# Retention and two feed-forward layers on one core: rooms for raw weight tiles, sums by DMA, scaling order

## The chip, the cores and the metric

The kernel runs on one core of one Trainium2 chip. The metric is the device time of one execution in microseconds. The core has a matrix engine (TensorE, PE in the rows, with its weight loads as PEld), a vector engine (VectorE, DVE), an activation engine (ScalarE, ACT), GpSimd (POOL), which here only issues DMAs, and SyncE (SP), which issues nearly all DMAs. Each engine works through its own queue in order and waits on semaphores.

## The reference

Everything is fp32. A retention (linear attention with a decaying state) over 4 batches, 8 heads, 768 positions and 64 features gives 3072 tokens of 512 features. They pass through two feed-forward layers of width 2048:

```python
state = gamma * state + k[t] (outer) v[t];  y[t] = scale * q[t] @ state
h = x @ w_in;  P = a0 + a1*h + a2*h**2 + a3*h**3
Q = 1 + |b0|*|h| + |b1|*h**2;  x = (P / (Q + 1e-6)) @ w_out        # layer 1
h = x @ w_in2;  out = (h * clip(h + 3, 0, 6) / 6) @ w_out2         # layer 2
```

## The kernel before

**Blocks and steps.** The 3072 tokens are cut into 6 blocks of 512 and the width 2048 into 16 units of 128. A step is one unit of one block in one layer: 96 steps per layer, 192 in all, written out one after the other (L653). Step n computes `h` of its unit with 12 matmuls (`emit_h`, L319), then the activation of the step before (`s1_h`, L393; `s1_pq`, L405; `s1_r`, L414; layer 2: `s2_h`, `s2_g`), the end of the activation of two steps before (`s1_g`, `s_hi`, `s_lo`), and last adds the result of two steps before into the accumulators of its block (`emit_o`, L331, 12 matmuls). fp32 accuracy comes from splitting every operand in two parts of the matrix engine's reduced fp32 type: xh and xl, gh and gl, and for weights the two halves of one `both` tile, hi and lo. The order of steps in layer 1 is block 0 units 0 to 7 (steps 0 to 7), block 1 units 0 to 15 (8 to 23), block 0 units 8 to 15 (24 to 31), then blocks 2 to 5; layer 2 has the same order.

**Attention.** Each block has four chunks of 128 tokens (`att_load` to `att_evac`). Block 0's run ahead of step 0. Block 1's are spread over steps 0 to 7, those of block 2 (VIA) over steps 8 to 22, one every four steps; their loads are issued at steps 7, 11, 15 and 19 into the tiles T, tq and kv, each once chunk c-1 has been read, and their result goes through DRAM (`x_via`). Blocks 0 and 1 (EARLY) have tiles a, b and r per chunk, 24 tiles in all, in the places that weights take later (`early_pair`).

**Weight tiles.** The weights of each layer are 32 tiles of 512 KB (wi and wo of 16 units), numbered by need: 0 = wi0, 1 = wi1, 2 = wo0, 3 = wi2, 4 = wo1 and so on; 16 and 17 are wi8 and wi9, 18 = wo8, 19 = wi10, 20 = wo9, 21 = wi11, up to 31; layer 2 has 32 to 63. A tile passes through these stages:

- `w_load` (L94): SP loads the raw tile into a room (L98 or L103; raw tiles are called rwi and rwo).
- `w_scale` (L109): ScalarE scales the upper half words in place (L111).
- `w_bits` (L115): VectorE puts the number together in three instructions (L119, L120, L123). L120 and L123 need the scaling; the trio is called the shift in this text.
- `w_hi` (L128): ScalarE writes hi (L131).
- lo = number minus hi, either by VectorE (L143), or for the tiles that `by_dma` names: ScalarE writes -hi into lo (`w_minus`, L135), and GpSimd issues a DMA that adds the number to it in place (L141). After it the room is free.

`w_first` does the shift and hi of a tile and calls the scaling of a later tile between them; `w_second` makes lo. Two tiles per step are made in steps 0 to 8 (0 to 2 ahead of them), one per step in steps 9 to 19 (tiles 21 to 31); `w_until` sets this. In the last 16 steps of layer 1 (80 to 95) the first tiles of layer 2 are made, one every second step. In a step VectorE's order is: lo of the last tile, the first shift, the activation of the step before, attention, the second shift; the lo of a tile stands at the beginning of the step after.

**Rooms.** Raw tiles lie in rooms: two `raw` tiles, and kv and T until step 5, when these go to block 2's attention (L694); at step 80 they come back. `w_ahead` (L507) issues loads at the end of each step while a room is free in the list; a load on SP's queue waits there until the lo of the tile that was in its room is done. The functions hold the limits: `w_scale_next(i + 2)` lets the scaling run one tile ahead of the shift, as far as the tile's load has been issued.

Of the kernel before, what the change touches and what calls it, by code (L numbers as in the profile page):

```python
# [7 lines left out]
F32 = mybir.dt.float32  # L8
F32R = mybir.dt.float32r
# [9 lines left out]
VIA = 2  # L19
CUT1, CUT2 = 8, 8  # L20
LAG = 2
SUMS = (3, 20)
WARM = 3
Q_CONST = 1.0 + 1e-6
LN_SCALE = 2.0**16
# [4 lines left out]
def tile_retention_moe_moe2(  # L30
# [19 lines left out]
    FT = DFF // 128  # L50
# [3 lines left out]

    ctx.enter_context(tc.manual_schedule())
    const = ctx.enter_context(tc.tile_pool(name="const", bufs=1))
    wts = ctx.enter_context(tc.tile_pool(name="wts", bufs=FT))
    raw_p = ctx.enter_context(tc.tile_pool(name="raw", bufs=2))
    x_p = ctx.enter_context(tc.tile_pool(name="xin", bufs=1))
    g_p = ctx.enter_context(tc.tile_pool(name="g", bufs=2))  # L60
# [24 lines left out]

    def pair_tile(tag, name):

        if tag == "raw":
            return raw_p.tile([128, 1024], F32, tag="raw", name=name)
        if tag == "T":  # L90
            return att.tile([128, 1536], F32, tag=tag, name=name)[:, 0:1024]
        return att.tile([128, 1024], F32, tag=tag, name=name)

    def w_load(tag, kind, layer, f):  # L94
        src = ((w_in1, w_in2) if kind == "wi" else (w_out1, w_out2))[layer].bitcast(I32)
        raw = pair_tile(tag, f"r{kind}{layer}_{f}").bitcast(I32)
        if kind == "wi":
            nc.sync.dma_start(  # L98
                out=raw.rearrange("p (c f) -> p c f", c=KD),
                in_=src[:, f * 256 : (f + 1) * 256].rearrange("(c p) f -> p c f", p=128),  # L100
            )
        else:
            nc.sync.dma_start(out=raw, in_=src[f * 128 : (f + 1) * 128, :])  # L103
        raws[kind, layer, f] = raw.rearrange("p (n t) -> p n t", t=2)
# [4 lines left out]
    def w_scale(kind, layer, f):  # L109
        hw = raws[kind, layer, f][:, :, 1].bitcast(F32)  # L110
        nc.scalar.activation(hw, hw, AF.Copy, scale=2.0**-112)  # L111
# [3 lines left out]
    def w_bits(kind, layer, f):  # L115
        raw = raws[kind, layer, f]
        lw, hw = raw[:, :, 0], raw[:, :, 1]
        z = raw.rearrange("p n t -> p (n t)")[:, 0:512]
        nc.vector.tensor_scalar(out=lw, in0=lw, scalar1=29, scalar2=None, op0=ALU.logical_shift_right)  # L119
        nc.vector.scalar_tensor_tensor(  # L120
            out=lw, in0=hw, scalar=-(2**31), in1=lw, op0=ALU.bitwise_and, op1=ALU.bitwise_or
        )
        nc.vector.scalar_tensor_tensor(  # L123
            out=z, in0=hw, scalar=3, in1=lw, op0=ALU.logical_shift_left, op1=ALU.bitwise_or
        )
        raws[kind, layer, f] = z.bitcast(F32)

    def w_hi(kind, layer, f):  # L128
        both = wts.tile([128, 1024], F32R, tag=kind, name=f"{kind}{layer}_{f}")
        weights[kind, layer, f] = (both[:, 0:512], both[:, 512:1024])  # L130
        nc.scalar.activation(weights[kind, layer, f][0], raws[kind, layer, f], AF.Copy)  # L131

    def w_minus(kind, layer, f):
        hi, lo = weights[kind, layer, f]
        nc.scalar.activation(lo, hi.bitcast(F32), AF.Copy, scale=-1.0)  # L135

    def w_lo(kind, layer, f, by_dma):
        hi, lo = weights[kind, layer, f]
        z = raws.pop((kind, layer, f))
        if by_dma:  # L140
            nc.gpsimd.dma_start(out=lo.bitcast(F32), in_=z, accum_op=ALU.add)  # L141
        else:
            nc.vector.tensor_tensor(out=lo, in0=z, in1=hi.bitcast(F32), op=ALU.subtract)  # L143
# [3 lines left out]
    loaded = {}  # L147
    attn = {}
    score = {}
    early = {"n": 0}  # L150

    def early_pair(name):

        early["n"] += 1
        tag = ("wi", "wo")[early["n"] % 2]
        return wts.tile([128, 1024], F32R, tag=tag, name=name).bitcast(F32)

    def heads(t):
        return t.rearrange("p (h d) -> p h d", h=H)
# [13 lines left out]
    def att_load(blk, c, parts=(0, 4, 1, 3, 2)):  # L173
        nm = f"{blk}_{c}"
        g = blk * CPB + c
        if (blk, c) not in loaded:
            if blk in EARLY:
                a, b, r = (early_pair(f"T{i}_{nm}") for i in "abr")
                q, tq, ka = a[:, 0:512], a[:, 512:1024], b
            else:  # L180
                t = att.tile([128, 1536], F32, tag="T", name=f"T{nm}")
                q, ka = t[:, 0:512], t[:, 512:1536]
                r = pair_tile("kv", f"kv{nm}")
                tq = att.tile([128, 512], F32, tag="tq", name=f"tq{nm}")
            loaded[blk, c] = [q, ka[:, 0:512], r[:, 0:512], r[:, 512:1024], tq, ka]
        for i in parts:
            if i == 4:
                src = tables[:, g % CPS * DM : (g % CPS + 1) * DM]
            else:
                src = (qk_t, kv)[i // 2][g, :, i % 2 * 512 : (i % 2 + 1) * 512]  # L190
            nc.sync.dma_start(out=loaded[blk, c][i], in_=src)
# [286 lines left out]
    def at_step(n):  # L478
        return steps[n] if 0 <= n < len(steps) else None
# [3 lines left out]
    for layer in range(2):  # L483
        need = []
        for f in range(FT):
            n = min(at_of[layer, b, f] for b in range(NBLK))
            need += [(n, "wi", layer, f), (n + LAG, "wo", layer, f)]
        jobs += [j[1:] for j in sorted(need, key=lambda j: j[0])]
    NW = 2 * FT
    made = {"load": 0, "scale": 0, "bits": 0, "lo": 0}  # L490
    free = ["raw", "raw", "kv", "T"]
    lent = {"kv": True, "T": True}
    held = {}

    def by_dma(i):
        return SUMS[0] <= i < SUMS[1]

    def w_until(n):

# [5 lines left out]
        return min(2 * NW, NW + 7 + (135 * (m + 1) + 99) // 100 if m < CUT2 else NW + 11 + m)  # L505

    def w_ahead(lim):  # L507
        while free and made["load"] < lim:
            i = made["load"]
            held[i] = free.pop(0)  # L510
            w_load(held[i], *jobs[i])
            made["load"] += 1

    def w_scale_next(lim):
        if made["scale"] < min(made["load"], lim):
            w_scale(*jobs[made["scale"]])
            made["scale"] += 1
# [3 lines left out]
    def w_first():  # L521
        i = made["bits"]
        if made["scale"] == i:
            w_ahead(i + 1)
            w_scale_next(i + 1)
        w_bits(*jobs[i])
        w_scale_next(i + 2)
        w_hi(*jobs[i])
        if by_dma(i):
            w_minus(*jobs[i])  # L530
        made["bits"] += 1

    def w_second():
        if made["lo"] < made["bits"]:
            i = made["lo"]
            w_lo(*jobs[i], by_dma(i))
            tag = held.pop(i)
            if lent.get(tag, True):
                free.append(tag)
            made["lo"] += 1  # L540


# [22 lines left out]
    for key in (VIA, *range(NBLK, 2 * NBLK)):  # L565
        n = at_of[0, key, 0] if key < NBLK else at_of[1, key - NBLK, 0]
# [58 lines left out]
    w_bits(*jobs[0])  # L625
    made["bits"] = 1
    w_hi(*jobs[0])
    att_q(0, 3)
    att_scores(0, 3)
# [23 lines left out]
    for n in range(len(steps) + LAG):  # L653
        cur, k1, k2 = (at_step(n - i) for i in range(3))
        todo = w_until(n) - made["bits"]
        if cur:
            emit_h(cur)
        for fn, *args in begun:
            fn(*args)
        begun.clear()  # L660
        if k1:
            (s1_h, s2_h)[k1[0]](k1)
        for key in late:
            if key[:2] not in partial and key[0] == 0:
                emit_evac(*key)
        for fn, *args in begin.get(n, ()):
            fn(*args)
        if k2 and k2[0] == 0:
            s1_g(k2)
            s_hi(k2)  # L670
        elif k2:
            s_lo(k2)
        for key in late:
            if key[:2] in acc:
                emit_evac(*key)
        late.clear()
        while made["lo"] < made["bits"]:
            w_second()
        rest = (lambda: s_lo(k2)) if k2 and k2[0] == 0 else None
        if k1 and k1[0] == 1:  # L680
            if rest:
                rest()
            s2_g(k1)
            s_hi(k1)
        if todo > 0:
            w_first()
        if k1 and k1[0] == 0:
            s1_pq(k1, rest)
            s1_r(k1)
        if todo > 1:  # L690
            w_second()
        for fn, *args in before.get(n, ()):
            fn(*args)
        if n == CUT1 - 3:  # L694
            lent.update(kv=False, T=False)
            free[:] = [t for t in free if t == "raw"]
        if n == N1 - FT:
            lent.clear()
            free += ["kv", "T"]
        if todo > 1:  # L700
            w_first()
        w_ahead(NW if n < N1 - FT else 2 * NW)
        o = at_step(n - LAG)
        if o:
            emit_o(o)
            if o[2] == ends[o][1]:
                late.append(o)
        for fn, *args in after.get(n, ()):
            fn(*args)
        if cur and cur[1:] == (0, FT - 1):  # L710
            sum_load(*cur[:2])
# [71 lines left out]
```

## Time and profile before

| | us |
|---|---|
| median of 3 runs | 1224.5 (1223.58 to 1227.64) |
| profiled execution, its own time | 1225.62 |
| its span, first to last instruction | 1223.6 |
| TensorE busy | 1158.8 (95%) |
| VectorE busy | 813.4 (66%) |
| ScalarE busy | 617.3 (50%) |
| GpSimd busy | 15.4 (1%), 23 instructions |

The shares are means over stretches that have different limits, so the rows below go by stretches. A row of an order of time gives start, duration, engine, line, operation, the tile written and the tiles read; the bracket at its end is the idle time of the engine before it and what ended that.

### The profile page before, as it was taken

The page shows a single profiled execution, that of the slowest core. Times are in us where ns is not written, and L with a number is a line of the kernel's source. Part 1 is how long each engine was busy: PE and PEld are TensorE (multiplying, and loading weights), DVE is VectorE, ACT ScalarE, POOL GpSimd, SP SyncE. Part 2 cuts the span into 40 slices and gives each one's busy share as a digit, 9 for nine tenths or more (in the row PEclk, how much of TensorE's full clock was granted, in tenths as well). Part 3 has the DMA queues.
Part 4 walks back from the last instruction along what each step waited for, and adds up shares of the span by engine and source line. Part 5 has one row for each costly group of instructions (what it writes and reads, how often), then busy time and mean ns, then how long its engine had stood idle before and what let it go on. Part 6 is the DMA issues. An engine that isn't in the chain of part 4 may idle for free.

```text
span 1223.6 us, 15677 instructions
## 1 busy us (share of the span) xinstructions
PE 1158.8 (95%) x6022; PEld 936.2 (77%) x6022; DVE 813.4 (66%) x1264; ACT 617.3 (50%) x1003; POOL 15.4 (1%) x23
## 2 busy tenths in 40 slices
PE   6776888999999999999999899999999999999998
PEld 5554666788888888888776688888888888888886
DVE  6897889999888888887899997643323232332222
ACT  2576656686666666655777665433222222222222
POOL 0111000000000000000000000000000000000000
PEclk8898899999999999999999999999999999999999
DMA  9776433231211221212121264302100100100000
GB/s 333 221 180 155 136 97 104 76 132 52 70 44 44 78 87 44 78 44 81 67 78 43 69 207 138 103 1 86 61 9 1 61 9 1 61 9 1 35 1 35
DMA packets 57099, 95.74 MB, mean 78 GB/s; under 512 B 5057, under 2 KB 23617, under 8 KB 57025
## 3 DMA queue, kind: packets, MB, share of 16 engines
q1 hardware_dynamic: 54576, 90.29, 22.5%
q0 software_dynamic: 2448, 4.46, 2.2%
q8 instruction: 47, 0.77, 0.3%
q14 instruction: 28, 0.22, 0.1%
HBM read 74.54 MB, written 15.73 MB: 74 GB/s over the span
## 4 chain that ended last, share of the span: by engine, by line
PE 74%; DVE 14%; ACT 4%; DMA 4%; issue 3%; SPq 0%; DVEq 0%; ACTq 0%; POOLq 0%
PE h L328 35%; PE accA L352 18%; PE accB L352 18%; DMA rwo<-in_moe_w_out_dram 2%; PE sc L216 1%; DVE p L408 1%; DVE u L423 1%; PE py L247 1%; DVE p L424 1%; DVE u L409 1%; DVE rwo L120 1%; DVE p L412 1%; DVE rwi L120 1%; DVE p L425 1%; DMA wi<-rwi 1%
## 5 line engine op out<-in xcount | busy, mean ns | idle before, releaser
L328 PE MATMUL h<-xh,wi 128*128 128x512 f32 x1536 | 418.7, 395 | 0.7 <-ACT xh L303 0.7
L328 PEld LDWEIGHTS h<-xh,wi 128*128 128x128 f32 x1536 | 287.2, 189 | 65.0 <-issue 3.2
L328 PE MATMUL h<-xl,wi 128*128 128x512 f32 x768 | 206.1, 390 | 0.0
L448 DVE SCALAR_TENSOR_TENSOR g<-r,h 128x512 f32<-128x512 f32 x96 | 66.0, 688 | 164.6 <-ACT r L442 164.1
L328 PEld LDWEIGHTS h<-xl,wi 128*128 128x128 f32 x768 | 144.7, 188 | 31.0
L442 ACT ACTIVATE r<-h,cst 128x512 f32<-128x512 f32 x96 | 65.9, 686 | 178.1 <-PE h L328 177.5
L352 PE MATMUL accA<-gh,wo 128*128 128x512 f32 x384 | 122.5, 401 | 20.7 <-ACT gh L430 20.7
L436 DVE TENSOR_TENSOR gl<-g,gh 128x512 fp32r<-128x512 f32 x96 | 66.4, 692 | 112.3 <-ACT gh L430 112.3
L430 ACT ACTIVATE gh<-g 128x512 fp32r<-128x512 f32 x96 | 60.8, 633 | 150.5 <-PE accB L352 116.6
L352 PE MATMUL accB<-gh,wo 128*128 128x512 f32 x384 | 120.8, 396 | 0.0
L352 PE MATMUL accA<-wo,gh 128*128 128x512 f32 x384 | 118.3, 389 | 0.0
L352 PE MATMUL accB<-wo,gh 128*128 128x512 f32 x384 | 118.2, 389 | 0.0
L352 PEld LDWEIGHTS accA<-gh,wo 128*128 128x128 f32 x384 | 71.5, 191 | 41.4 <-ACT gh L430 26.6
L417 ACT ACTIVATE r<-u,cst 128x512 f32<-128x512 f32 x96 | 69.3, 722 | 54.6 <-DVE u L409 54.6
L400 ACT ACTIVATE p<-h,ab 128x512 f32<-128x512 f32 x96 | 74.3, 774 | 38.9 <-PE h L328 36.7
L436 DVE TENSOR_TENSOR gl<-p,gh 128x512 fp32r<-128x512 f32 x96 | 65.7, 685 | 32.3 <-ACT gh L430 32.1
L352 PEld LDWEIGHTS accB<-gh,wo 128*128 128x128 f32 x384 | 73.6, 192 | 15.8
L352 PEld LDWEIGHTS accA<-wo,gh 128*128 128x128 f32 x384 | 72.1, 188 | 15.0
L352 PEld LDWEIGHTS accB<-wo,gh 128*128 128x128 f32 x384 | 72.1, 188 | 14.9
L352 PE MATMUL accA<-gl,wo 128*128 128x512 f32 x192 | 64.2, 410 | 19.0 <-DVE gl L436 18.6
L430 ACT ACTIVATE gh<-p 128x512 fp32r<-128x512 f32 x96 | 60.7, 632 | 34.7 <-DVE p L425 34.6
L352 PE MATMUL accB<-wo,gl 128*128 128x512 f32 x192 | 74.8, 389 | 0.0
(77 smaller groups left out, 1468.3 us busy)
## 6 DMA issues: line engine op xcount, KB each, us to landing
rwi<-in_moe_w_in_dram SPq DMA_DIRECT2D x32, 512.0 KB, 3.8
rwo<-in_moe_w_out_dram SPq DMA_DIRECT2D x32, 512.0 KB, 3.5
T<-in_qk_t_dram SPq DMA_DIRECT2D x32, 256.0 KB, 3.9
kv<-in_kv_dram SPq DMA_DIRECT2D x32, 256.0 KB, 4.5
x<-o SPq DMA_DIRECT2D x24, 256.0 KB, 2.3
xr<-x SPq DMA_DIRECT2D x24, 256.0 KB, 3.7
out_dram<-o SPq DMA_DIRECT2D x20, 256.0 KB, 2.1
Tr<-in_kv_dram SPq DMA_DIRECT2D x16, 256.0 KB, 6.2
```

The costliest lines, as they stand in the source:

```text
L120: nc.vector.scalar_tensor_tensor(out=lw, in0=hw, scalar=-(2**31), in1=lw, op0=ALU.bitwise_and, op1=ALU.bitwise_or)
L216: nc.tensor.matmul(banks[e][:, p * CH : (p + 1) * CH], lhsT=kT[rows, p, :], rhs=qT[rows, p, :], start=True, stop=True)
L247: nc.tensor.matmul(to(e, j, i), lhsT=vr[:, 2 * p + e, :], rhs=am[:, e * NP + p, :], start=j == 0, stop=first and j == 1, skip_group_check= ...
L328: nc.tensor.matmul(ps, lhsT=w[:, cs], rhs=x[:, c, :], start=n == 0, stop=n == 3 * KD - 1)
L352: nc.tensor.matmul(acc[layer, blk][j], lhsT=l, rhs=r, start=f == f0 and i == 0, stop=f == f1 and i == 2)
L400: nc.scalar.activation(p, h, AF.Identity, scale=ab[:, 3:4], bias=ab[:, 2:3])
L408: nc.vector.tensor_tensor(out=p, in0=p, in1=h, op=ALU.mult)
L417: nc.scalar.activation(r, u, AF.Ln, scale=1.0 / LN_SCALE, bias=ln_bias)
L430: nc.scalar.activation(gh, tm[key], AF.Copy)
L436: nc.vector.tensor_tensor(out=gl, in0=tm.pop(key), in1=gh.bitcast(F32), op=ALU.subtract)
L442: nc.scalar.activation(r, hps[key], AF.Relu, bias=three)
L448: nc.vector.scalar_tensor_tensor(out=g, in0=r, scalar=6.0, in1=h, op0=ALU.min, op1=ALU.mult)
```

## The change

All weights have a place of their own: the pool had 16 buffers for wi and 16 for wo, used in turn, and has one each for 32 tags (wi0 to wo15). The early attention tiles lie in fixed places, from unit 8 on, and block 1's chunk c takes those of block 0's chunk c. The places of the last two units (wi14, wo14, wi15, wo15) hold raw tiles for loads 0 to 23, beside the two `raw` tiles: six rooms; kv and T are rooms only from step 80 on. Lo by DMA is used for tiles 3 to 25 and 32 to 39 (31 tiles) in place of 3 to 19 (17). `w_first` lets the scaling run up to i + 3, and after step 1 one more scaling is called, which puts it two tiles ahead of the shift.

```diff
-SUMS = (3, 20)
+SUMS = ((3, 26), (32, 40))
+EARLY_AT = 8
+SPARE, SPARE_TO = ("wi14", "wo14", "wi15", "wo15"), 24
-    wts = ctx.enter_context(tc.tile_pool(name="wts", bufs=FT))
+    wts = ctx.enter_context(tc.tile_pool(name="wts", bufs=1))
     def pair_tile(tag, name):
+        if tag in SPARE:
+            return wts.tile([128, 1024], F32R, tag=tag, name=name).bitcast(F32)
     def w_hi(kind, layer, f):
-        both = wts.tile([128, 1024], F32R, tag=kind, name=f"{kind}{layer}_{f}")
+        both = wts.tile([128, 1024], F32R, tag=f"{kind}{f}", name=f"{kind}{layer}_{f}")
-    def early_pair(name):
-        early["n"] += 1
-        tag = ("wi", "wo")[early["n"] % 2]
-        return wts.tile([128, 1024], F32R, tag=tag, name=name).bitcast(F32)
+    def early_pair(c, i, name):
+        n = 2 * EARLY_AT + 3 * c + i
+        return wts.tile([128, 1024], F32R, tag=f"{('wi', 'wo')[n % 2]}{n // 2}", name=name).bitcast(F32)
-    free = ["raw", "raw", "kv", "T"]
-    lent = {"kv": True, "T": True}
+    free = [*SPARE, "raw", "raw"]
     def by_dma(i):
-        return SUMS[0] <= i < SUMS[1]
+        return any(lo <= i < hi for lo, hi in SUMS)
     def w_ahead(lim):
-        while free and made["load"] < lim:
+        while made["load"] < lim:
             i = made["load"]
-            held[i] = free.pop(0)
+            rooms = [t for t in free if i < SPARE_TO or t not in SPARE]
+            if not rooms:
+                return
+            held[i] = rooms[0]
+            free.remove(rooms[0])
     def w_first():
...
-        w_scale_next(i + 2)
+        w_scale_next(i + 3)
     def w_second():
...
-            tag = held.pop(i)
-            if lent.get(tag, True):
-                free.append(tag)
+            free.append(held.pop(i))
...
-        if n == CUT1 - 3:
-            lent.update(kv=False, T=False)
-            free[:] = [t for t in free if t == "raw"]
         if n == N1 - FT:
-            lent.clear()
             free += ["kv", "T"]
         if todo > 1:
             w_first()
         w_ahead(NW if n < N1 - FT else 2 * NW)
+        if n == 1:
+            w_scale_next(NW)
```

## Rows read from the trace of the kernel before

**Rows 1.** Stretches: us, length, busy time and instructions per engine, clock, DMA.
```profile
29.58:107.30 77.72, 59.71 (x393) 45.15 (x393) 71.65 (x115) 54.71 (x94) 13.35 (x15) 0.91 0.75 197
107.30:160.00 52.70, 36.44 (x181) 27.04 (x179) 39.79 (x66) 29.95 (x50) 1.76 (x2) 0.84 0.49 145
160.00:240.00 80.00, 72.34 (x424) 55.50 (x425) 73.59 (x117) 50.10 (x83) 0.00 (x0) 0.96 0.26 80
240.00:600.00 360.00, 360.00 (x2111) 293.72 (x2110) 310.42 (x477) 235.28 (x381) 0.00 (x0) 1.00 0.21 69
600.00:700.00 100.00, 91.22 (x385) 70.15 (x384) 93.15 (x148) 71.30 (x119) 0.00 (x0) 1.00 0.20 64
```

**Rows 2.** Chain of waits, 95 to 160 us: start, us, what.
```profile
101.92 6.56 DMA wi<-rwi
108.53 3.58 DMA rwo<-in_moe_w_out_dram
...
134.75 2.56 PE accB L352 x6
...
150.47 5.53 DMA rwo<-in_moe_w_out_dram
```

**Rows 3.** VectorE in order of time, 104 to 160 us.
```profile
112.21 0.43 DVE L119 TENSOR_SCALAR rwo<-rwo 128x512 int32<-128x512 int32 x1 [4.50 <-DMA rwo<-in_moe_w_out_dram]
...
116.23 0.59 DVE L119 TENSOR_SCALAR rwi<-rwi 128x512 int32<-128x512 int32 x1
118.54 0.69 DVE L120 SCALAR_TENSOR_TENSOR rwi<-rwi 128x512 int32<-128x512 int32 x1 [1.72 <-ACT rwi L111]
...
127.46 0.68 DVE L143 TENSOR_TENSOR wo<-rwo,wo 128x512 fp32r<-128x512 f32 x1
128.63 0.44 DVE L119 TENSOR_SCALAR rwi<-rwi 128x512 int32<-128x512 int32 x1 [0.49 <-DMA rwi<-in_moe_w_in_dram]
...
139.53 0.69 DVE L120 SCALAR_TENSOR_TENSOR rwo<-rwo 128x512 int32<-128x512 int32 x1 [3.04 <-ACT rwo L111]
...
146.51 0.68 DVE L143 TENSOR_TENSOR wo<-rwo,wo 128x512 fp32r<-128x512 f32 x1
...
148.59 0.69 DVE L120 SCALAR_TENSOR_TENSOR rwi<-rwi 128x512 int32<-128x512 int32 x1 [1.06 <-ACT rwi L111]
...
156.03 0.43 DVE L119 TENSOR_SCALAR rwo<-rwo 128x512 int32<-128x512 int32 x1 [0.57 <-DMA rwo<-in_moe_w_out_dram]
```

**Rows 4.** GpSimd in order of time, the accumulating DMA of tile 12.
```profile
83.17 0.90 POOL L141 DMA_DIRECT2D wo<-rwo  x1 [5.82 <-ACT wo L135]
```

**Rows 5.** DMA issues: tile, queue, count, KB each, median us to landing.
```profile
wo<-rwo POOLq DMA_DIRECT2D x8, 256.0 KB, 4.4
```

**Rows 6.** Chain of waits, 0 to 300 us: one subtraction.
```profile
220.72 0.60 DVE wo L143
```

**Rows 7.** Line 135: count, ns min/median/max, first and last start.
```profile
L135 ACT ACTIVATE wi<-wi x9: 630/632/636, 37.5 to 120.7; 128x512 fp32r<-128x512 f32 x9
```

**Rows 8.** All engines in order of time, 606 to 622 us: ScalarE's logarithm.
```profile
618.95 0.72 ACT L417 ACTIVATE r<-u,cst 128x512 f32<-128x512 f32 x1 [0.69 <-DVE u L409]
```

**Rows 9.** TensorE in order of time, 128 to 152 us.
```profile
132.67 0.79 PE L352 MATMUL accA<-gl,wo 128*128 128x512 f32 x1 [2.87 <-DVE gl L436]
...
144.66 1.09 PE L247 MATMUL py<-T,kv 128*64 128x128 f32 x16
```

**Rows 10.** One stretch more (step 9), columns as in rows 1.
```profile
122.91:138.92 16.01, 10.37 (x41) 7.28 (x39) 12.39 (x21) 10.50 (x19) 0.00 (x0) 0.68 0.39 117
```

**Rows 11.** Chain of waits, 0 to 300 us: six matmuls at full clock.
```profile
252.98 1.36 PE accA L352 x6
```

**Rows 12.** Groups of VectorE and TensorE, 604 to 699 us: count, busy, mean ns, idle before.
```profile
L143 DVE TENSOR_TENSOR wi<-rwi,wi 128x512 fp32r<-128x512 f32 x5 | 3.4, 683 | 0.0
L143 DVE TENSOR_TENSOR wo<-rwo,wo 128x512 fp32r<-128x512 f32 x4 | 2.7, 685 | 0.0
L352 PE MATMUL accA<-gl,wo 128*128 128x512 f32 x30 | 10.3, 423 | 7.0 <-DVE gl L436 7.0
```

More of the change, by code (lines that the diff above doesn't have):

```diff
@@ L149, in tile_retention_moe_moe2 @@
     score = {}
-    early = {"n": 0}
-    def early_pair(name):
-        early["n"] += 1
-        tag = ("wi", "wo")[early["n"] % 2]
-        return wts.tile([128, 1024], F32R, tag=tag, name=name).bitcast(F32)
+    def early_pair(c, i, name):
+        n = 2 * EARLY_AT + 3 * c + i
+        return wts.tile([128, 1024], F32R, tag=f"{('wi', 'wo')[n % 2]}{n // 2}", name=name).bitcast(F32)
     def heads(t):
@@ L177, in att_load @@
             if blk in EARLY:
-                a, b, r = (early_pair(f"T{i}_{nm}") for i in "abr")
+                a, b, r = (early_pair(c, i, f"T{i}_{nm}") for i in range(3))
                 q, tq, ka = a[:, 0:512], a[:, 512:1024], b
```

## The prediction

> **What bounds the kernel now.** I read the table of stretches first [rows 1]. From 240 to 600 us TensorE is busy for all of 360.00 us, so nothing can be won there; 29.58 to 107.30 has VectorE at 71.65 of 77.72; 107.30 to 160 has neither (TensorE 36.44, VectorE 39.79 of 52.70): somebody waits for something else; 160 to 240 and 600 to 700 have VectorE at 73.59 of 80 and 93.15 of 100, with TensorE idle for 7.7 and 8.8 us. The change touches weight preparation, which lies in just these stretches. So I look for two things: the waits of 107 to 160, and VectorE's work elsewhere.
>
> The chain of waits names the first [rows 2]: an accumulating DMA (6.56 us) gives a room back, then a weight tile is loaded (3.58 us), and VectorE stands still. VectorE's own order of time gives the sizes [rows 3]: 4.50 us for the load of tile 18, 1.72 for the scaling of tile 19, 0.49 for the load of tile 21, 3.04 and 1.06 for the scaling of tiles 22 and 23, 0.57 for the load of tile 24. These waits begin where only two rooms are left, since kv and T are withdrawn at step 5.
>
> **Rooms (tiles 0 to 23).** With six rooms used in turn, the load of tile i waits for tile i-6 instead of i-2. Tile 18 waits today for the accumulation of tile 16, which leaves at 101.92 and gives the room at 108.48 [rows 2]; it would wait for that of tile 12, issued at 83.17 [rows 4] and landed some 4.4 us later [rows 5], so near 88. Its load then lands by 95 even at the 5.53 us of the slowest load on the chain, and VectorE wants it at 107.7. The 4.50 us go. The same margin holds for tiles 19 to 23: tile 22 waits for the room of 16, free at 108.5, and has landed by 114.1; its scaling stands behind the shift of tile 20, which precedes that tile's subtraction (127.46 today) by some 4 us, so near 117 once 6.2 us are gone. What is late next is worked out below. The load of tile 24 is not helped: from 24 on only the two raw rooms count, and they hold 22 and 23.
>
> **Scaling two ahead.** ScalarE works in order, and today's scaling of tile 19 stands behind the three activations of `s1_h`; two tiles ahead it is done a half step or more earlier. So the wait of 1.72 goes, and 3.04 and 1.06 as well. It adds no instruction, only moves one activation to the end of step 1, where ScalarE has slack (54.71 us busy of 77.72 [rows 1]). If the load is not there, ScalarE waits, and behind it are `w_hi`, `s1_h`, `gh` and the exponential, and VectorE and TensorE behind those: the last rival. From tile 24 the limit is what has been loaded, and the order falls back to that of today; in layer 2 the scaling is one ahead before and after.
>
> **Fourteen more sums by DMA.** Each takes one subtraction off VectorE, 0.60 us on the chain [rows 6], and adds one activation on ScalarE (0.63 us [rows 7]), one issue on GpSimd (0.90 [rows 4]) and a transfer of 256 KB landing in 4.4 us. GpSimd has nothing else queued. On ScalarE the activation stands before the logarithm, which waits for VectorE's u for 0.69 us as a rule after `w_hi` [rows 8]; 0.63 fits into that, at most 0.1 is left over per tile. The room comes free with the DMA where today it comes with a subtraction in the next step. At tile 22 today: the second of three shift instructions starts at 139.53, the subtraction ends near 147.2 [rows 3]; by DMA the two last shift instructions (1.4), `w_hi` and `w_minus` (1.3) and the landing (4.4) would give 146.6. That is the same time, so I put it at 0, with bounds: a landing of 6.56 instead of 4.4 is 2.2 us late, and four loads (24 to 27) have little lead: up to 9 us lost; nothing gained. Behind such a load on SP's queue stand the next step's attention loads and stores, for which block 2's attention waits.
>
> VectorE's shift beside GpSimd's issue takes 0.59 against 0.43 us [rows 3] (tile 19 against tiles 18 and 24). Six more issues near it: 0 to 1.0 us, taken 0.6. The Trainium skill speaks against this part of the change: its page SBUF — State Buffer says (section "SBUF: two separate sides") that a DMA of GpSimd's queue is held up while VectorE runs an instruction that takes both ports, because its descriptors can't be written, and (section "A bandwidth-pool intuition that's wrong") gives 620 ns growing to 3100, by which each added sum would land some 2.5 us later. The trace agrees as to VectorE's side (the 0.16 us); on the DMA's side today's sums land in 4.4 us beside a VectorE that is busy more than nine tenths of the time, so what delay there is lies in that figure. What late sums would cost here is the rival of the late rooms, worked out from the 6.56 us alone.
>
> **What the places do.** They hold the same bytes. Block 1's chunks take the places of block 0's. TensorE is done with block 0's attention when step 0 starts at 29.58, and the loads of block 1 follow two or more chunks behind their readers: nothing.
>
> **The sum, stage by stage.** *107 to 132.* Waits of 4.50 + 1.72 + 0.49 and one subtraction (tile 20, at 127.46), 0.60: 7.3 us, all on VectorE's way to the `gl` which starts TensorE's work at 132.67 [rows 9].
>
> *132 to 156: here most of the rest is lost.* The 3.04 and 1.06 us and the subtractions of tiles 21 to 23 are 5.9 us on VectorE, but from 132.67 to the attention matmuls at 144.66 TensorE is busy without a gap [rows 9] (the rows between these two show no idle time). Behind those matmuls come, on SP's queue, the store to `x_via`, five attention loads and only then the load of tile 24, 5.53 us, at 150.47 [rows 2]. VectorE would only come earlier to that load and wait some 3 us instead of 0.57. What can shorten this part is the clock: it is granted at 0.68 from 122.91 to 138.92 [rows 10], since TensorE had waited; six matmuls take 2.56 us there [rows 2] and 1.36 at full clock [rows 11]. Ten of them at the half clock cost 10 x 0.2 = 2.0 us. Whether two waits of some 3 us per step still bring the clock down is open: 0 to 2.0, taken 1.0.
>
> *156 to 240.* Tiles 24 and 25 lose a subtraction each on a saturated VectorE: 1.2, less 0.1 for the logarithm: 1.1 (bounds: minus 9, the late rooms, to 1.2).
>
> *604 to 699.* VectorE runs nearly without a gap; TensorE waits 7.0 us for `gl` [rows 12]. Nine subtractions lie there (5 and 4 rows); the last, tile 40, stays. Eight go: 8 x 0.60 = 4.8 us. TensorE's idle 8.8 us are more than that, so all of it can come out (0 if the waits belong to ScalarE instead).
>
> Together 7.3 + 1.0 + 1.1 + 4.8 - 0.6 = 13.6 us. The profiled execution took 1225.6 (span 1223.6 and 2.0 around it), 1.1 above the median of 1224.5: 1212.0 for such an execution, 1210.9 for the median.
>
> **The rivals.** *The rooms come late:* the accumulations of tiles 22 to 25 land late, and loads 24 to 27 hold VectorE up, 9 us lost: 13.6 - 9 = 4.6, so 1219.9. For it: the 6.56 us on the chain; against: medians of 4.4, and most of a step of lead, as from step 9 on a step makes one tile.
>
> *More comes out:* TensorE keeps the full clock through 107 to 140 and the half step's waits close, 2.0 instead of 1.0, and the 5.9 us of 132 to 156 come out for 4 us, since the attention of block 2 also moves forward: 13.6 + 1.0 + 4 = 18.6, so 1205.9. Against it stands the gapless TensorE of [rows 9].
>
> *It doesn't do what it says:* rooms are there but SP's queue, held by waits for other sums, issues the loads no earlier: the subtractions alone, 1.1 + 4.8 + 0.6 - 0.6 = 5.9, so 1218.6.
>
> *Slower:* ScalarE stands still for loads. Scaling tile i+2 in order pays if its load has landed; if it lands later than the `s1_h` before it, every step from 1 to 9 has such a wait, sixteen tiles (8 to 23). One wait of 1.6 us each (not quite half of a load of 3.58) is 26 us: 1224.5 + 26 - 13.6 = 1236.9. It decides from the point where the load of a tile is issued less than about 4 us before its scaling. Against: rooms of i-6 give a step or more.
>
> **How the numbers follow.** Forecast 0.60 (1210.9, itself 1207 to 1214); late rooms 0.13; more 0.12; not what it says 0.08; slower 0.07. A measurement of this kernel can tell 0.3%, 3.7 us, from no change. All cases but the last lie below 1220.8, though the late rooms can double: faster 0.87, same 0.06, slower 0.07. The range takes in the forecast, both cases of partial gain and that of more: 1204 to 1220.
>
> **What would show it.** Right: VectorE's 4.50, 1.72, 3.04 and 1.06 us waits gone; loads 18 to 23 issued 10 us or more ahead of their shift; a wait of 2 to 4 us for tile 24; TensorE's waits for `gl` in the last 100 us of layer 1 down from 7.0 to about 3. Wrong: ScalarE waiting for loads (L111), VectorE waiting for tiles 25 to 27, TensorE idle as before around 600 to 700.

## The result, and the profile after

The changed kernel takes 1211.74 us (median; 1210.76 to 1215.67) beside 1225.16 of the kernel before in the same session: a ratio of 0.9895, 95% interval 0.9867 to 0.9923. The prediction was 1210.9 in a range of 1204 to 1220. The profiled execution took 1212.05 us, with a span of 1210.1, where the one of before had 1225.62 and 1223.6; from profile to profile 13.5 us went, and the sum had 13.6.

The stretches again, between the same times as [rows 1] (us, length, busy time and count of TensorE, its weight loads, VectorE, ScalarE and GpSimd, granted clock, DMA share, GB/s):

```profile
29.58:107.30 77.72, 61.84 (x397) 47.05 (x396) 72.33 (x117) 55.14 (x94) 13.40 (x15) 0.89 0.83 216
107.30:160.00 52.70, 41.14 (x199) 31.50 (x199) 43.73 (x70) 36.20 (x62) 6.70 (x8) 0.87 0.58 150
160.00:240.00 80.00, 73.32 (x438) 56.76 (x437) 71.96 (x114) 51.69 (x85) 0.28 (x1) 0.98 0.28 86
600.00:700.00 100.00, 96.95 (x411) 75.90 (x411) 94.98 (x152) 77.56 (x130) 6.03 (x7) 1.00 0.39 108
```

TensorE does 4.7 us more in the second stretch and 5.7 more in the last, and only 1.0 more from 160 to 240, where VectorE was to lose two subtractions. But stretches between fixed times mix steps, since the work behind the first gain moves forward. So I cut both traces at the starts of steps (a step begins with its first matmul into `h`); the last line is the difference:

| us | start of step 0 | steps 0 to 8 | 8 to 24 | 24 to 82 | 82 to 98 | 98 to 191 |
|---|---|---|---|---|---|---|
| before | 29.58 | 77.72 | 137.36 | 357.09 | 100.27 | 505.92 |
| after | 28.46 | 77.09 | 130.45 | 357.09 | 95.42 | 505.92 |
| gone | 1.12 | 0.63 | 6.91 | 0 | 4.85 | 0 |

Two of these four gains were in the sum: steps 8 to 24 and 82 to 98. Of the first two columns more below.

VectorE of after in order of time (start, duration, engine, line, operation; in the bracket the idle time before and what ended it). Lines of after lie 5 lower in the weight functions and 3 lower further down: L124, L125 and L128 are the shift, L148 the subtraction, L439 `gl`, L116 the scaling.

```profile
105.84 0.42 DVE L124 TENSOR_SCALAR rwo<-rwo 128x512 int32<-128x512 int32 x1
109.63 0.53 DVE L124 TENSOR_SCALAR rwi<-rwi 128x512 int32<-128x512 int32 x1
...
129.23 0.69 DVE L439 TENSOR_TENSOR gl<-p,gh 128x512 fp32r<-128x512 f32 x1 [0.32 <-ACT gh L433]
...
139.62 0.69 DVE L426 SCALAR_TENSOR_TENSOR u<-u,r 128x512 f32<-128x512 f32 x1 [0.78 <-ACT r L421]
147.23 0.43 DVE L124 TENSOR_SCALAR rwo<-rwo 128x512 int32<-128x512 int32 x1 [5.53 <-DMA rwo<-in_moe_w_out_dram]
...
156.31 0.69 DVE L125 SCALAR_TENSOR_TENSOR rwi<-rwi 128x512 int32<-128x512 int32 x1 [0.92 <-ACT rwi L116]
163.78 0.69 DVE L125 SCALAR_TENSOR_TENSOR rwo<-rwo 128x512 int32<-128x512 int32 x1 [0.91 <-ACT rwo L116]
...
595.47 0.69 DVE L125 SCALAR_TENSOR_TENSOR rwi<-rwi 128x512 int32<-128x512 int32 x1 [3.17 <-ACT rwi L116]
```

The waits of [rows 3] for tiles 18 to 23 are gone: tile 18 (105.84) has no bracket, nor has tile 19. In their place stands one wait of 5.53 us, for the load of tile 24. New are 0.92 and 0.91 us at tiles 25 and 26, for the scaling.

The loads on SP's queue, tile 18's, tile 22's, the store to `x_via`, tiles 24 and 25, and GpSimd's sum of tile 23:

```profile
86.19 0.34 SPq L108 DMA_DIRECT2D rwo<-in_moe_w_out_dram  x1
104.52 0.33 SPq L108 DMA_DIRECT2D rwo<-in_moe_w_out_dram  x1
136.63 0.37 SPq L302 DMA_DIRECT2D x_via<-xf  x1
139.57 0.39 SPq L108 DMA_DIRECT2D rwo<-in_moe_w_out_dram  x1
145.89 0.38 SPq L103 DMA_DIRECT2D rwi<-in_moe_w_in_dram  x1
```
```profile
138.60 0.86 POOL L146 DMA_DIRECT2D wi<-rwi  x1 [7.06 <-ACT wi L140]
```

Tile 18's load is issued 19.65 us ahead of VectorE; the one of tile 24 comes 2.94 us behind the store, as before (147.51 to 150.47), and is 7.66 us from its issue to VectorE's first instruction on it, where before it was 5.56 (150.47 [rows 2] to 156.03 [rows 3]).

TensorE, in order of time, and its group that answers to the last of [rows 12] (601 to 696 us):

```profile
122.96 0.79 PE L355 MATMUL accA<-gl,wo 128*128 128x512 f32 x1 [1.44 <-DVE gl L439]
133.78 1.09 PE L250 MATMUL py<-T,kv 128*64 128x128 f32 x16
151.26 1.22 PE L355 MATMUL accA<-gl,wo 128*128 128x512 f32 x2 [5.11 <-DVE gl L439]
598.80 0.73 PE L355 MATMUL accA<-gl,wo 128*128 128x512 f32 x2 [1.02 <-DVE gl L439]
```
```profile
L355 PE MATMUL accA<-gl,wo 128*128 128x512 f32 x30 | 10.4, 421 | 1.8 <-DVE gl L439 1.8
```

Over steps 82 to 98 TensorE waits 2.8 us for `gl` (1.8 in this group and the 1.02 at 598.80, which lies ahead of it), where it was 7.0.

### The profile page after: what moved, and what is told of

Same layout as the page of the kernel before. It is cut to its first block, busy times and chain, and to the rows that moved or that the text cites. A ratio compares the mean times of both kernels' runs of the same rounds, so it can differ in the third digit from the quotient of the medians.

```text
span 1210.1 us, 15716 instructions
## 1 busy us (share of the span) xinstructions
PE 1158.3 (96%) x6022; PEld 937.0 (77%) x6022; DVE 805.6 (67%) x1250; ACT 624.5 (52%) x1017; POOL 27.6 (2%) x37
## 4 chain that ended last, share of the span: by engine, by line
PE 74%; DVE 5%; ACT 2%; issue 1%; ACTq 0%; DVEq 0%
PE h L331 36%; PE accA L355 18%; PE accB L355 18%; PE sc L219 1%; PE py L250 1%; DVE u L426 1%; DVE u L412 1%; DVE p L411 1%; DVE p L427 1%; PE py L276 1%; ACT r L420 0%; ACT r L421 0%; DVE p L415 0%; PE py L262 0%; DVE p L428 0%
## 5 line engine op out<-in xcount | busy, mean ns | idle before, releaser
L439 DVE TENSOR_TENSOR gl<-g,gh 128x512 fp32r<-128x512 f32 x96 | 66.5, 692 | 112.3 <-ACT gh L433 112.3
L439 DVE TENSOR_TENSOR gl<-p,gh 128x512 fp32r<-128x512 f32 x96 | 65.9, 686 | 32.9 <-ACT gh L433 32.7
L355 PE MATMUL accA<-wo,gl 128*128 128x512 f32 x192 | 74.7, 389 | 0.0
```

The costliest lines, as they stand in the source:

```text
L355: nc.tensor.matmul(acc[layer, blk][j], lhsT=l, rhs=r, start=f == f0 and i == 0, stop=f == f1 and i == 2)
L439: nc.vector.tensor_tensor(out=gl, in0=tm.pop(key), in1=gh.bitcast(F32), op=ALU.subtract)
```

## The experiments

All times are medians; each ratio is to the kernel before on the same chip, whose median was 1225.16 to 1226.20 us in the five sessions. The segments of all traces, in us:

| run | step 0 at | 0 to 8 | 8 to 24 | of it 12 to 13 | 82 to 98 |
|---|---|---|---|---|---|
| before | 29.58 | 77.72 | 137.36 | 8.16 | 100.27 |
| after | 28.46 | 77.09 | 130.45 | 11.67 | 95.42 |
| e1_sums_only | 26.92 | 78.93 | 137.55 | 9.71 | 95.43 |
| e2_rooms_only | 29.90 | 77.74 | 130.08 | 9.40 | 101.53 |
| e3_rooms_scale | 26.91 | 77.97 | 129.18 | 9.74 | 101.86 |
| e4_rooms_sums | 29.93 | 77.69 | 131.59 | 11.65 | 95.40 |
| e6_sums_split | 26.62 | 78.25 | 130.16 | 9.99 | 95.42 |
| e13_not_23 | 31.83 | 77.12 | 128.53 | 9.12 | 95.43 |
| e5_spare28 | 26.78 | 78.20 | 121.31 | 5.54 | 95.42 |
| e8_scale32 | 27.15 | 78.09 | 130.51 | 11.80 | 93.81 |
| e9_changed_again | 26.96 | 78.42 | 131.18 | 11.68 | 95.40 |
| e10_one_ahead_again | 30.06 | 77.71 | 130.83 | 11.68 | 95.41 |
| e11_best | 26.98 | 78.19 | 121.57 | 5.83 | 93.77 |
| e12_best_sums_split | 28.66 | 77.08 | 123.28 | 5.48 | 93.76 |

Steps 24 to 82 take 357.09 or 357.10 in all of them. The other stretch, 98 to 191, takes 505.92, but for 506.27 in e2_rooms_only and 505.94 in e3_rooms_scale.

The rows after and e9_changed_again are two traces of one kernel. They differ by 1.50 us in the start of step 0, by 1.33 in steps 0 to 8 and by 0.73 in steps 8 to 24, so a difference of that size between two kernels says nothing in these columns. In steps 12 to 13 and 82 to 98 they agree to 0.02.

### The three parts, one and two at a time

**e1_sums_only**: the kernel before, with the 31 sums alone.

```diff
-SUMS = (3, 20)
+SUMS = ((3, 26), (32, 40))
...
-        return SUMS[0] <= i < SUMS[1]
+        return any(lo <= i < hi for lo, hi in SUMS)
```

> The kernel before with lo by DMA for tiles 3 to 25 and 32 to 39, rooms and scaling as before. Theory (a sum pays only where VectorE is what ends last): the last 100 us of layer 1 lose 4.8 us (the after trace has 13.5 - 8.7 = 4.8 there), the first 240 us at most 1, since VectorE waits there for loads and scalings: 5 us, about 1219.5. Rival 1 (each subtraction off VectorE counts): 14 x 0.60 = 8.4 us, 1216. Rival 2 (late sums hold rooms back where two rooms are left): the first 240 us get slower by 2 to 5 us, about 1222 to 1224.

Measured: 1220.10 us (1219.52 to 1221.04), ratio 0.9955 [0.9938, 0.9972]. All of the gain that is in the work lies in steps 82 to 98; steps 8 to 24 are not shorter at all. VectorE loses six subtractions there (busy 114.26 us instead of 118.06), and its waits grow by as much, from 18.72 to 22.69 us in all. The large ones, at tiles 18, 19 and 22, stay as they are together, and others grow: the one for the load of tile 24 is 1.93 instead of 0.57. These are the three large ones, together 9.22 us, which answer to 4.50, 1.72 and 3.04 in [rows 3], together 9.26:

```profile
110.00 0.43 DVE L119 TENSOR_SCALAR rwo<-rwo 128x512 int32<-128x512 int32 x1 [3.73 <-DMA rwo<-in_moe_w_out_dram]
...
116.35 0.69 DVE L120 SCALAR_TENSOR_TENSOR rwi<-rwi 128x512 int32<-128x512 int32 x1 [1.90 <-ACT rwi L111]
...
137.72 0.69 DVE L120 SCALAR_TENSOR_TENSOR rwo<-rwo 128x512 int32<-128x512 int32 x1 [3.59 <-ACT rwo L111]
```

**e2_rooms_only**: the rooms alone; the changed kernel with

```diff
-SUMS = ((3, 26), (32, 40))
+SUMS = ((3, 20),)
...
-        w_scale_next(i + 3)
+        w_scale_next(i + 2)
...
-        if n == 1:
-            w_scale_next(NW)
```

> The changed kernel with the 17 sums of before and the scaling one tile ahead as before: only places and six rooms. Theory 1 (the scaling fell behind before only because loads were late; with loads there, one tile ahead is enough): VectorE's waits of 4.50, 1.72, 3.04 and 1.06 us go all the same, gain 7 us in the first 240, nothing near 600: about 1217. Theory 2 (the recorded reason: the scaling must go two ahead to take away 1.72, 3.04 and 1.06): the 4.50 and 0.49 go, the others stay: about 1219.5.

Measured: 1219.48 us (1216.95 to 1220.89), ratio 0.9947 [0.9926, 0.9968]. The rooms alone shorten steps 8 to 24 by 7.28 us, and VectorE has no wait above 0.21 us from 100 us to the load of tile 24. So the waits for scaling (1.72, 3.04, 1.06) go without scaling two ahead: the scaling had been late because the loads were. In the last steps of layer 1 nothing is gained (101.53 against 100.27; here the clock fell once, below).

**e3_rooms_scale**: the changed kernel with the 17 sums of before, `SUMS = ((3, 20),)`.

> The changed kernel with the 17 sums of before: rooms and scaling two ahead. Both theories: 7 us in the first 240, about 1217; by theory 1 the same as with rooms alone within 1 us, by theory 2 some 2.5 us faster than that. The last 100 us of layer 1 as before, TensorE waiting 7.0 us for gl.

Measured: 1216.70 us (1216.60 to 1216.78), ratio 0.9926 [0.991, 0.9942]. That is 2.78 less than e2_rooms_only, but from step 0 to 191 the two traces are 0.67 apart (1172.05 and 1172.72 us); step 0 begins 2.99 earlier here.

**e4_rooms_sums**: the changed kernel with the scaling one ahead, the last three edits of e2_rooms_only without that of `SUMS`.

> The changed kernel with the scaling one tile ahead as before. Theory 1: as the changed kernel within 1 us, 1211.7. Theory 2: waits of 1.72 and more for scalings come back at tiles 19 to 23, some 2.5 us slower, 1214.

Measured: 1215.41 us (1214.16 to 1216.06), ratio 0.9915 [0.9895, 0.9935]. With e2_rooms_only this shows the sums' two places apart: 82 to 98 falls from 101.53 to 95.40, 8 to 24 rises from 130.08 to 131.59, all of it behind step 12 (92.90 to 94.59 us in steps 12 to 24).

### The six sums of tiles 20 to 25

**e6_sums_split**: the changed kernel without them: `SUMS = ((3, 20), (32, 40))`.

> The changed kernel with sums by DMA for tiles 3 to 19 and 32 to 39, so without the six of tiles 20 to 25. Theory (off the path: VectorE only reaches the load of tile 24 earlier, and pays for ScalarE's extra activations): same or up to 1.5 us faster, 1210.2 to 1211.7. Rival (the recorded step: tiles 20, 24 and 25 gain 0.6 each): 1.7 us slower, 1213.4.

Measured: 1211.88 us (1211.06 to 1213.00), ratio 0.9883 [0.9868, 0.9899]; the changed kernel has 1211.74 and 1211.85. Six of the fourteen new sums bring nothing on balance. Two things are seen in the trace. First, load 24: with tile 23's sum, whose issue stands some 1 us ahead of that load, five traces (after, e4, e8, e9, e10) have 7.62 to 7.77 us from the load's issue to VectorE's first instruction on it; without it three (e2, e3, e6) have 5.97 to 6.17. In e1_sums_only, where this sum is issued 1.22 us behind the load, it is 6.30. Second, tiles 25 and 26. Here is VectorE with the subtraction in place (L148, 0.60 to the next start), then ScalarE of after at the same place:

```profile
154.23 0.68 DVE L148 TENSOR_TENSOR wo<-rwo,wo 128x512 fp32r<-128x512 f32 x1
154.83 0.43 DVE L124 TENSOR_SCALAR rwi<-rwi 128x512 int32<-128x512 int32 x1
155.58 0.70 DVE L125 SCALAR_TENSOR_TENSOR rwi<-rwi 128x512 int32<-128x512 int32 x1 [0.32 <-ACT rwi L116]
```
```profile
155.09 0.63 ACT L433 ACTIVATE gh<-p 128x512 fp32r<-128x512 f32 x1 [1.34 <-DVE p L428]
155.63 0.65 ACT L116 ACTIVATE rwi<-rwi 128x512 f32<-128x512 f32 x1
```

The scaling of tile 25 stands behind `gh` on ScalarE, and `gh` waits for VectorE's p. With the subtraction VectorE waits 0.32 us for that scaling; without it 0.92 (above): exactly the 0.60 that were saved. The subtraction had been lying beside `gh` and the scaling.

**e13_not_23**: the changed kernel with the sum of tile 23 alone taken back: `SUMS = ((3, 23), (24, 26), (32, 40))`.

> The changed kernel with the sum of tile 23 alone taken back to VectorE (30 sums). Five traces with that sum have its issue about 1 us ahead of the load of tile 24 and 7.6 to 7.8 us from that load's issue to VectorE's first instruction on the tile; three without it have 6.0 to 6.2 us. Theory 1: the transfer of that sum lies beside the load and costs it 1.65 us. Then the load takes 6.0 to 6.2 us here, VectorE's wait for it falls from 5.53 to about 4.4 (1.65 less, 0.6 more since one subtraction is back and VectorE comes later), and step 24 begins 1 to 1.7 us earlier against step 0; time 0.5 to 1.7 us below the changed kernel's 1211.85. Theory 2: it is the sums of tiles 22 or 24, or the number of sums in all; then 7.6 us stay, and the time is within 0.5 us of the changed kernel's.

Measured: 1210.44 us (1209.15 to 1213.88), ratio 0.9884 [0.9866, 0.9903]. SP's loads of tiles 24 and 25, and VectorE:

```profile
143.12 0.38 SPq L108 DMA_DIRECT2D rwo<-in_moe_w_out_dram  x1
145.23 0.38 SPq L103 DMA_DIRECT2D rwi<-in_moe_w_in_dram  x1
```
```profile
148.99 0.43 DVE L124 TENSOR_SCALAR rwo<-rwo 128x512 int32<-128x512 int32 x1 [3.82 <-DMA rwo<-in_moe_w_out_dram]
```

5.87 us instead of 7.66, and the wait is 3.82 instead of 5.53. The sum of tile 23 alone did it. Its 256 KB lie beside the load: in the changed kernel it is issued at 138.60 and lands 7.24 us later, and in this time the DMA engines are busy throughout (the next to last number, 0.99, is their share). The row shows it; that the sum takes from the load what it needs of these engines is inferred, since the edit shows what the sum costs, not how.

```profile
138.60:145.84 7.24, 7.24 (x34) 5.92 (x32) 2.28 (x4) 3.32 (x6) 0.86 (x1) 1.00 0.99 256
```

The sum also gave its room late: load 25 follows load 24 by 2.11 us here and by 6.32 with the sum. Steps 8 to 24 are 128.53, which is 1.9 to 2.7 less than in the three traces of the changed kernel and its like (130.45, 130.51, 131.18). Part of that lies ahead of the load; steps 12 to 24 alone take 92.49 us here and 94.04 to 94.65 in the five traces with the sum. In the time only 1.4 show, and the ranges overlap: this profiled execution has its step 0 at 31.83, the latest of all.

### What the changed kernel still loses

**e5_spare28**: six rooms for loads 24 to 27 too; the diff to the changed kernel:

```diff
-SPARE, SPARE_TO = ("wi14", "wo14", "wi15", "wo15"), 24
+SPARE, SPARE_TO = ("wi14", "wo14", "wi15", "wo15"), 28
```

> The changed kernel with the four spare places open to loads 0 to 27 instead of 0 to 23 (tile 24 in wi14, 25 in wo14, 26 in wi15, 27 in wo15; 28 and 29 find the raw tiles free). Theory (what the changed kernel still loses between 132 and 156 us is the load of tile 24, behind block 2's attention loads on SP's queue): VectorE's wait of 5.53 us goes, and the 0.9 us waits for scalings of tiles 25 and 26 with it; some 5 us in all and up to 3 more at tile 28: 1204 to 1207. Rival (TensorE, gapless from 123 to 141 us, sets the pace, and the load only fills its time): within 1 us of 1211.7.

Measured: 1203.83 us (1202.21 to 1204.74), ratio 0.9816 [0.9799, 0.9832], 8 us below the changed kernel. VectorE comes to tile 24 at 141.48 without a wait, and the stretch of [rows 1] is

```profile
141.48 0.42 DVE L124 TENSOR_SCALAR rwo<-rwo 128x512 int32<-128x512 int32 x1
```
```profile
107.30:160.00 52.70, 44.80 (x237) 34.45 (x236) 49.56 (x80) 42.40 (x72) 6.98 (x8) 0.94 0.71 182
```

Steps 12 to 13 fall from 11.67 to 5.54 us, and the clock is granted at 0.94 where it was 0.87.

**e8_scale32**: the changed kernel, with one more scaling called ahead of layer 2's first tile:

```diff
+        if n == N1 - FT + 1:
+            w_scale_next(NW + 1)
```

> The changed kernel with the scaling of tile 32 called at the end of step 81 instead of inside step 82, where it stands behind the four evacuations of block 4's accumulators. VectorE's wait of 3.17 us (L125 at 595.47) goes. Theory (layer 1's last 100 us are bound by VectorE, TensorE waiting 0.3 to 1.0 us for gl every second step): up to 3 us faster, 1209. Rival (TensorE is nearly full there by now, 96.95 of 100 us, and it sets the pace): within 1 us.

Measured: 1210.71 us (1210.09 to 1212.14), ratio 0.9877 [0.9859, 0.9895]. In the time that is 1.0 below the changed kernel, with ranges that overlap. Steps 82 to 98 take 93.81, 1.6 less: half of the 3.17 us at 595.47, since VectorE then waits for the next thing that ScalarE makes:

```profile
597.71 0.69 DVE L426 SCALAR_TENSOR_TENSOR u<-u,r 128x512 f32<-128x512 f32 x1 [1.61 <-ACT r L421]
```

**e11_best** (e5_spare28 and e8_scale32 together), and **e12_best_sums_split** (the same without the sums of tiles 20 to 25).

> The changed kernel with spare places for loads 0 to 27 and the scaling of tile 32 in step 81. Gains of different stages add: 8 + 1.6 us, 1202.

> The kernel with both additions, but without the six sums by DMA of tiles 20 to 25. Theory (a sum pays where VectorE ends last; with tile 24's load early VectorE does from 140 to 215 us): slower by 0.6 us for each of tiles 22 to 25, some 2 to 3 us, 1204 to 1205. Rival (ScalarE's extra activations eat it as in the changed kernel): within 1 us of 1202.

Measured: 1201.67 us (1200.64 to 1204.66), ratio 0.9806 [0.9788, 0.9824], and 1203.22 (1202.78 to 1203.38), ratio 0.9814 [0.9799, 0.9829]. The two gains add, and e11_best is 24 us below the kernel before. With load 24 out of the way the six sums bring 1.7 us in steps 8 to 24 (121.57 against 123.28), 1.55 in the medians, though the ranges overlap.

### Scaling two ahead, and the time ahead of step 0

**e9_changed_again** is the changed kernel once more, **e10_one_ahead_again** is e4_rooms_sums once more, both on one chip.

> The changed kernel once more, beside the next three on one chip: 1211 to 1213, the base for them.

> The changed kernel with the scaling one tile ahead, as in the run before, now beside the changed kernel. Theory 1 (once loads are early, one tile ahead is enough; the 3.7 us between the medians are the clock of the part ahead of step 0, which lies at 28.5 in the one trace and 29.9 in the other): within 1.5 us of the changed kernel. Theory 2 (two ahead carries part of the gain): 3 to 4 us slower, as the medians said.

Measured: 1211.85 us (1211.38 to 1212.49), ratio 0.9884 [0.9867, 0.99], and 1213.71 (1213.38 to 1214.59), ratio 0.9901 [0.9887, 0.9916]. The ranges don't touch, so the 1.86 us between the medians are more than either's spread. But in the traces they don't lie where the scaling is moved: from step 0 to 191 the two take 1168.02 and 1166.97 us (the segments and 24 to 82 and 98 to 191 added up), so one ahead is 1.1 shorter; it begins 3.10 later. Ahead of step 0 both kernels issue the same instructions. What differs there is the clock. The first row is e9_changed_again, the second e10_one_ahead_again (columns as in [rows 1]):

```profile
10.00:30.00 20.00, 13.80 (x230) 11.43 (x226) 16.88 (x28) 6.10 (x11) 0.00 (x0) 1.00 1.05 374
```
```profile
10.00:30.00 20.00, 13.98 (x220) 12.19 (x216) 13.88 (x22) 4.24 (x8) 0.00 (x0) 0.83 1.04 373
```

Three traces with one ahead (e2, e4, e10) begin at 29.90 to 30.06, those with two ahead at 26.6 to 28.7, as if the cause were the order of scaling. e13_not_23 speaks against it: two ahead, and 31.83. And e1_sums_only, one ahead, begins at 26.92. Why the medians of e9 and e10 differ is left open, and with it the 2.78 us between e2 and e3, which has the same sign. That scaling two ahead shortens the steps as a whole is not shown. It does shorten one way, from VectorE's first instruction on tile 18 to TensorE's `gl`: 17.10 to 17.12 us in after, e8 and e9, and 17.37 and 17.38 in e4 and e10. And part of an early start is lost again in steps 0 to 8, with either order: in e9_changed_again ScalarE waits 1.99 us for a load there, in e1_sums_only (one ahead, 26.92) 1.90, in e10 not at all.

```profile
37.48 0.70 ACT L116 ACTIVATE rwo<-rwo 128x512 f32<-128x512 f32 x1 [1.99 <-DMA rwo<-in_moe_w_out_dram]
```

## Why the prediction was right, and where its steps were not

**The rooms: right, 7.84 instead of 7.3.** From VectorE's first instruction on tile 18 (without its wait) to TensorE's `gl` matmul the way was 24.96 us (107.71 to 132.67 [rows 9]) and is 17.12 (105.84 to 122.96). The load's time, predicted as near 88, is 86.19; tile 22's, predicted 108.5, is 104.52. e2_rooms_only gives 7.16 of it by itself (107.95 to 125.75 is 17.80); with the sums the way is 17.37 (e4_rooms_sums), with the scaling two ahead too 17.12.

**Scaling two ahead: the result right, the reason wrong.** I put 1.72, 3.04 and 1.06 us to its account; e2_rooms_only removes them without it. They were the late loads' too. What scaling two ahead adds on this way is the 0.25 us between 17.37 and 17.12.

**The clock, 1.0 taken: 1.17 here, 0.01 in the second trace, so luck.** From `gl` to the attention matmuls it was 11.99 us (132.67 to 144.66) and is 10.82 (122.96 to 133.78), at a granted clock of 0.84 instead of 0.76. In e9_changed_again, the same kernel, it is 11.98 us at 0.75. The rows of before, after and e9_changed_again:

```profile
132.67:144.66 11.99, 11.99 (x50) 9.14 (x50) 8.69 (x14) 8.61 (x16) 0.00 (x0) 0.76 0.40 133
```
```profile
122.96:133.78 10.82, 10.82 (x50) 8.38 (x51) 10.15 (x16) 9.32 (x17) 1.53 (x2) 0.84 0.55 147
```
```profile
122.76:134.74 11.98, 11.98 (x51) 9.19 (x51) 11.21 (x18) 9.29 (x17) 1.51 (x2) 0.75 0.50 133
```

**The load of tile 24: named rightly, 2.1 us too cheap.** I wrote that VectorE would only come earlier to that load and wait some 3 us (2 to 4). It waits 5.53, because the load itself takes 7.66 instead of 5.56. The failed step is the price of the added sums: I counted each one's own landing and put the rest at 0, and did not count that its transfer lies beside a load that is waited for. e13_not_23 shows that it costs 1.8 (7.66 to 5.87). The Trainium skill's page SBUF — State Buffer (sections "SBUF: two separate sides" and "A bandwidth-pool intuition that's wrong"), weighed in the prediction, warns of DMAs of GpSimd's queue that are held up beside VectorE; 2.5 us for each sum was the prediction's estimate from its 620 and 3100 ns. The runs do not show such a delay: the sums land in a median of 4.8 and 3.7 us, where 17 had 4.0 (x9) and 4.4 [rows 5] (all 31 in a median of 3.9, the 17 in 4.3), and tile 23's, which took 7.24 us, had VectorE busy for only 2.28 us beside it (row of e13_not_23 above). The medians:

```profile
wi<-rwi POOLq DMA_DIRECT2D x17, 256.0 KB, 4.8
wo<-rwo POOLq DMA_DIRECT2D x14, 256.0 KB, 3.7
```

**156 to 240 us: wrong, 1.1 predicted, nothing found.** From VectorE's first instruction on tile 24 to the u of step 23 (L409, now L412) 88.59 us became 88.73. I read "VectorE 73.59 of 80" [rows 1] as a saturated engine, from which each instruction taken away comes out. It was a chain that goes from VectorE to ScalarE and back: the subtraction lay beside `gh` and the scaling (e6_sums_split), and the 0.60 came back as a wait.

**VectorE beside GpSimd: 0.6 taken, 0.1 found.** The first shift instruction takes 0.53 or 0.54 us instead of 0.42 or 0.43 at tiles 17, 19 (109.63 above) and 21; at 17 and 19 it was 0.53 and 0.59 before, so only tile 21 is new.

**604 to 699: right, 4.85 for 4.8.** Eight subtractions less, TensorE's wait for `gl` 2.8 for "about 3". e1_sums_only gives it by itself, to 0.01 us. Why was the same reckoning right here and wrong at 156 to 240? Here nothing on ScalarE lay in VectorE's way behind the subtraction: its waits in steps 82 to 98, all for ScalarE, are 5.66 us before and 5.54 after. Where there was such a thing, at tile 32, taking 3.17 us away brought 1.6 (e8_scale32).

**The sum.** For steps 8 to 24 the prediction has 7.3 + 1.0 + 1.1 - 0.6 = 8.8 us; 6.91 came: 7.84 for the rooms and the sum of tile 20, 1.17 for the clock, 2.10 lost at load 24, 0.14 lost behind it, and 0.14 in the short stretches between. That the total was right to 0.1 is partly luck: 1.12 us ahead of step 0 and 0.63 in steps 0 to 8 were in no term, and the first is the clock, which changes from run to run of the same instructions. Without these 1.75 the profile would show 11.8. e9_changed_again, the same kernel, has 2.62 us ahead of step 0, 0.70 lost in steps 0 to 8, and 6.18 in steps 8 to 24.

**The rivals.** Late rooms (1219.9) had the right place, the sums' transfers against the loads, at a fifth of the price. "More comes out" did not happen in this kernel, since load 24 shut it off; e5_spare28, which takes that load away, gives 1203.83 against its 1205.9. "It doesn't do what it says" is excluded by the 86.19, and "slower" by ScalarE, whose only wait of more than 1 us for a load in these steps is the one for tile 24 (in e9_changed_again one more, the 1.99 us at 37.48, which goes with its early start and not with the order of scaling).

## What to carry to other kernels

Count an instruction taken off a busy engine as gain only where the next instruction on it does not wait for another engine that got its input ahead of it; a busy share of nine tenths does not tell these apart, and the order of time around one such place does. When a wait for rooms is removed, work out which transfer is first without a room now, and what else is in flight beside it: here that one load kept 8 us, as much as the rooms had brought. And move transfers off the moment at which a load is waited for, even where each of them is quick.

## What the runs showed of the hardware that was not expected

The clock ahead of step 0 differs between runs with the same instructions there, and the start of step 0 goes with it. In 10 to 30 us the granted clock is 1.00 in the seven traces where step 0 begins at 26.62 to 27.15 us, 0.91 in two (28.46 and 28.66), 0.83 in four (29.58 to 30.06) and 0.77 in e13_not_23 (31.83). In e13_not_23 five executions lie at 1209.15, 1209.35, 1210.44, 1213.39 and 1213.88; the profiled one is the 1213.39. Its row:

```profile
10.00:30.00 20.00, 14.27 (x208) 12.88 (x204) 14.39 (x22) 3.65 (x6) 0.00 (x0) 0.77 1.03 369
```

The 5 us between the earliest and the latest start are more than most edits here are worth, so a gain of 2 us is to be sought in the steps, not in the time alone. The steps scatter too, where the clock falls in them: steps 8 to 12 take 35.91 us in after and 37.03 in e9_changed_again, the same kernel.

In the two experiments without sums in layer 2, steps 82 to 98 became longer than before (101.53 and 101.86 against 100.27), though VectorE had the same instructions to do; the clock fell there, which it did in these steps in no other trace. Why is open. In e3_rooms_scale:

```profile
690.00:695.00 5.00, 5.00 (x18) 3.98 (x17) 4.74 (x8) 4.43 (x9) 0.00 (x0) 0.75 0.38 147
```

A load of 512 KB that stands behind five attention loads took 5.56 to 6.17 us to VectorE in five traces, 6.30 with an accumulating DMA of 256 KB issued 1.2 us behind it (e1_sums_only), and 7.62 to 7.77 with one issued 1 us ahead of it (five traces).
